# Spreading the count of passed thresholds by VectorE turns in the later searches of a routed feed-forward kernel

## Chip, cores and metric

One core of a Trainium2 chip runs the whole program. The metric is device time in microseconds (us), the median of several runs. TensorE is called PE here, VectorE DVE, ScalarE ACT, GpSimd POOL, SyncE SP.

## What is computed

Attention over 8 batches, 8 heads, 576 positions and 64 features, in which scores more than tau under the row's maximum are dropped, feeds a mixture of 8 experts. Tokens (4608, 512 features) go to experts greedily by the largest logits, with room for 576 tokens in each expert:

```python
scores = scale * np.matmul(q, k.transpose(0, 1, 3, 2))
scores = np.where(scores >= np.max(scores, -1, keepdims=True) - tau, scores, -1e9)
x = softmax(scores) @ v                      # as (4608, 512)
logits = x @ w_gate                          # (4608, 8)
for idx in np.argsort(-logits.flatten()):    # greedy
    tok, e = idx // 8, idx % 8
    if assigned[tok] >= 0 or counts[e] >= 576: continue
    assigned[tok] = e; counts[e] += 1
for e in range(8):
    h = np.maximum(x[assigned == e] @ w1[e], 0.0)
    out[assigned == e] = h @ w2[e]
```

## The kernel before

The attention takes the first half of the time. Then eight rounds follow, each for the expert that fills up next: a search finds the threshold at which some expert has 576 takers among the tokens that are left, the tokens of that expert are compacted into a list, gathered from memory (`xg`), scaled and transposed by PE (`turn`, L821, into `pt`), split into a high and a low part (`xh` by ACT, `xl` by DVE), and go through two layers of matmuls (L880 for the first, L912 for the second) with weights that are split in the same way (`w1h`, `w1l`, `w2h`, `w2l`; the low parts are DVE subtractions). The hidden layer `H` is split as well. Round r+1's search runs beside round r's or round r-1's matmuls.

A search has seven levels, -1 to 5. At each, `step_cmp` compares all 128x36 best logits with up to 32 thresholds (DVE, `cmp`, 1152 columns); `step_cnt` counts them by expert in nine small matmuls (L496) and takes the counts out of PSUM (`cn`, or from the fourth search on four small DVE operations on `cs`); `step_flag` sets a flag for each threshold that some expert passes with at least 576 (`jka`, written as a column of `fla`: one flag on each of the first 32 partitions); `step_n` needs the number of flags, on all 128 partitions. It gets it by a PE product of `fla` with a matrix of ones (L545, levels -1 and 0) or with `hb`, which holds the width of a level's step (L531, levels 1 to 5), into the PSUM tile `rps`. DVE reads it there: at levels -1 and 0 in `jk`, which picks the threshold out of `E`, and at levels 1 to 4 in `sd`, the running sum of steps that the next level's `cmp` adds. The first search (`alone`) runs at the end of the attention and uses other PSUM tiles; searches 2 and 3 (`s.count<=ADDS`, ADDS is 3) sum the counts by another PE product; searches 4 to 7 sum them on DVE. The eighth round needs no search.

The order of instructions on each engine is fixed when the program is built. A planner holds a clock for PE (advanced by fixed amounts for each matmul of the feed-forward, plus `held` for products of the search) and, in the class `Vec`, one for DVE (each operation adds a time by its size). The search is a generator: where it yields `gap()`, the planner goes on placing feed-forward matmuls on PE until `V.wait()` has passed, that is until DVE's planned work is done plus a margin `V.lat`, which is `LATS[r]` for the search of round r (counted from 0; the third search has LATS[2]). At each gap, `s.fill()` puts one deferred DVE subtraction (`w1l`, `w2l`, low part of `H`) into DVE's queue; others are put there when they are older than AGE (7 us of the planner's clock), or when a matmul that needs them is placed. So at run time each engine works its own queue in order, and waits where the planner's clocks were off. The gather of a round's tokens goes to POOL's queue, the loads of weights to SP's. The `x` of round r is made once round r-1's first layer is done and 8 us (6.5 in round 1) of the planner's clock after the gather was issued; the search of round 2 stands still from round 1's `take` until round 1's `x` is done.

Of the kernel before, what the change touches and what calls it, by code (L numbers as in the profile page):

```python
# [9 lines left out]
F32 = mybir.dt.float32  # L10
F32R = mybir.dt.float32r
BF16 = mybir.dt.bfloat16
I32 = mybir.dt.int32
AF = mybir.ActivationFunctionType
ALU = mybir.AluOpType
AX = mybir.AxisListType
# [395 lines left out]

class Vec:

    def __init__(s,e): s.e=e; s.free=0.0; s.now=0.0; s.lat=LAT; s.fix=0.125
    def after(s,t): s.free=max(s.free,t)
    def ease(s): return max(0.0,s.free-s.now-0.4)
    def wait(s): return max(0.0,s.free-s.now)+s.lat
    def __getattr__(s,n):
        f=getattr(s.e,n)  # L420
        def g(out,*a,**k):
            src=k.get("in_",a[0] if a else out)
            big=max((int(np.prod(x.shape[1:])) for x in (out,src) if hasattr(x,"shape")),default=1)
            s.free=max(s.free,s.now)+s.fix+big/(0.96 if n!="tensor_tensor" or out.dtype!=BF16 or src.dtype!=BF16 else 1.9)/1000
            return f(out,*a,**k)  # L425
        return g
LAT=0.25

class Router:
# [77 lines left out]
    def step_flag(s,lv):  # L507

        V=s.V
        if s.count>ADDS: n=s.cn[:,3]  # L510
        else:
            n=s.ps()[0:32,0:8]
            if s.count>2: s.T.matmul(n,s.sum,s.cn,start=True,stop=True)
            else:
                for c in range(4): s.T.matmul(n,s.eye[:,32*c:32*c+32],s.cn[:,8*c:8*c+8],start=(c==0),stop=(c==3))
        if lv==1: V.tensor_scalar(s.st,s.st,s.lo,None,op0=ALU.add)
        jk=s.wk.tile([32,9],BF16,name="jka"); s.jk=jk; m=s.js
        fl=jk[:,8:9] if lv==5 else s.fl[0:m,lv+1:lv+2]
        V.tensor_scalar(jk[0:m,0:8],n[0:m],CAP-0.5,None,op0=ALU.is_ge,op1=ALU.max,accum_out=fl)
    def step_n(s,B):  # L520

        V=s.V
        lv=B["lv"]
        ps=s.ps()
        if lv>0:


            d=ps[:,0:1]
            for l in range(lv,0 if s.alone else lv-1,-1):
                k=32 if l==5 else 128  # L530
                s.T.matmul(d,s.hb[0:k,l-1:l].to_broadcast([k,128]),s.jk[:,8:9] if l==5 else s.fl[:,l+1:l+2],start=(l==lv),stop=(l==1 or not s.alone))  # L531
            if not s.alone and lv<5:
                sd=s.wk.tile([128,1],F32,name="sd",bufs=3)
                if lv==1: V.tensor_copy(sd,d)
                else: V.tensor_tensor(sd,B["add"],d,op=ALU.add)
                d=sd
            if lv<5: return {"add":d,"lv":lv+1}
            s.T.matmul(ps[:,1:10],s.ones[0:32],s.jk,start=True,stop=True)
            lo=s.wk.tile([128,1],F32,name="lo5",bufs=2)
            if s.alone: V.tensor_tensor(lo,s.lo,d,op=ALU.add)  # L540
            else: V.scalar_tensor_tensor(lo,d,B["add"],s.lo,op0=ALU.add,op1=ALU.add)
            return {"lo":lo,"lv":6,"full":ps}
        E2=s.wk.tile([128,J+2],F32,name="E",bufs=3)
        n=ps[:,0:1]
        s.T.matmul(n,s.ones,s.fl[:,lv+1:lv+2],start=True,stop=True)  # L545
        sm=s.wk.tile([128,2],F32,name="sm",bufs=3); lo=sm[:,0:1]
        jk=s.wk.tile([128,J+2],F32,name="jk2")
        V.scalar_tensor_tensor(jk,s.k("io"),n,B["E"],op0=ALU.is_equal,op1=ALU.mult,accum_out=lo)
        if lv==-1:

            V.tensor_scalar(E2,s.k("pw"),lo,FMAX,op0=ALU.mult,op1=ALU.min)
            V.scalar_tensor_tensor(E2,s.k("nw"),lo,E2,op0=ALU.mult,op1=ALU.max)
        else:
            s.ab=sm[:,1:2]
            V.scalar_tensor_tensor(s.ab,lo,-1.0,lo,op0=ALU.mult,op1=ALU.max)
            V.tensor_scalar(E2,s.k("io4"),s.ab,lo,op0=ALU.mult,op1=ALU.add)
        return {"E":E2,"lo":lo,"lv":lv+1}
# [86 lines left out]
    def phase(s,last=False):  # L644

        s.stage="search"; V=s.V
        def held(t): s.pe=t; V.after(V.now+t+0.2)
        if s.first: s.prep(31)
        else:
            yield V.ease()  # L650
            s.prep()
            yield V.ease()
        s.alone=s.first; s.first=False
        s.count+=1
        if last:

            lo=s.wk.tile([128,1],F32,name="lo"); V.memset(lo,-FMAX/4); E={"lo":lo}
        else:
            E={"E":s.k("E1"),"lv":-1}
            def gap():  # L660

                w=V.wait(); s.fill()
                return w
            s.on=True
            for i in range(7):
                s.step_cmp(E); yield gap()
                held(0.34); s.step_cnt(); yield gap()
                if s.count<=ADDS: held(0.16)
                s.step_flag(E["lv"]); yield gap()
                held(0.1); E=s.step_n(E)  # L670
                if not s.alone: yield V.ease()
            s.on=False
        s.pick(E)
        if last:
            yield V.wait()
            held(0.13); s.pick2()
        s.stage="pick"; s.rank1(E)
        yield V.wait()
        held(0.2); s.rank2()
# [14 lines left out]
        yield V.wait() if alone else 0.35  # L694
        s.idx=s.compact2(cps)

LATS=[0.15,0.35,0.7]+[0.8]*5; FIX=(0.125,0.15)
GA=[5.0,6.5,8.0,8.0]; AGE=7.0; HALF=1; WARM=[30,6,64]
W1Y=1.0; W1X=8.5; L2O=(0,4,1,2,3); L2Z=1; HFB=3; RW=[0.2,0.4,0.4,0.4]; LOWP=(); LPF=7; LOWT=1.4; PREPW=1; WLY=(1.0,1.0)

def moe(ctx,tc,R,start,xrows,w1,w2,out,ident):
    nc=tc.nc
    V=R.V; A=nc.scalar; G=nc.gpsimd; T=nc.tensor
    E,D,F=w1.shape
# [16 lines left out]
    def flush():  # L721
        while True:
            if fills and (clk[0]-fills[0][0]>AGE or (not R.on and V.free<=clk[0]+0.2)): pull()
            yield 0.3
# [63 lines left out]
    def rows(r,s):  # L788
        while r>0 and ("x",r-1) not in done: yield 0.5
        order=(4,0,1,2,3) if 0<r<=HALF else range(5)  # L790
        for t in order:
            n=128 if t<4 else 64
            x=wk.tile([128,XW],F32,name="xg",bufs=5); s["xg",t]=x
# [17 lines left out]
        def parts(t):  # L811
            ps=s["xps",t]
            if r==0: return (lambda n: s[n][:,:,128*t:128*t+128] if t<4 else s[n][:,:,512:576]),ps if t<4 else ps[:,:,:64]
            if t<4: return (lambda n: s[n][:,:,128*t+32*(t//2):128*t+32*(t//2)+128]),ps
            return (lambda n: s[n].rearrange("p k (a b) -> p k a b",a=2)[:,:,:,256:288]),ps[:,:,:64].rearrange("p k (a b) -> p k a b",a=2)
        def turn(t):
            n=128 if t<4 else 64
            ps=R.cp().rearrange("p (d n) -> p d n",d=4) if r==0 and t==4 else pt.tile([128,4,128],F32,name="pt")
            s["xps",t]=ps
            held[0]+=0.5  # L820
            for d in range(4): T.transpose(ps[:,d,:n],s["xg",t][:n,d*128:(d+1)*128],ident[:n,:n])  # L821
            xv,pv=parts(t); A.activation(xv("xh"),pv,AF.Copy)  # L822
        def low(t):
# [106 lines left out]
    def place():  # L930
        for r in range(8):
            while r>2 and ("l2",r-3) not in done: yield 0.5
            s=st[r]={}
            if r==0: yield start[1]
            V.now=clk[0]; V.lat=LATS[r]; V.fix=FIX[r>0]
            def steps(g):
                for d in g:
                    held[0]+=R.pe+(0.09 if R.pe else 0.0); R.pe=0.0
                    yield d
                    while ("take",1) in done and ("x",1) not in done: yield 0.2  # L940
                    V.now=clk[0]
                    if R.stage=="pick" and "ei" not in s:
                        s["ei"]=R.e
                        jobs.append([clk[0],w1_load(r,s)]); jobs.append([clk[0]+0.1,w2_load(r,s)])
                held[0]+=R.pe+(0.09 if R.pe else 0.0); R.pe=0.0
                if "ei" not in s:
                    s["ei"]=R.e
                    jobs.append([clk[0],w1_load(r,s)]); jobs.append([clk[0]+0.1,w2_load(r,s)])
            yield from steps(start[0] if r==0 else R.ahead if r==1 else R.phase(r==7))
            if r<2:  # L950
                yield from packing(r,s)
                while "ahead" not in done: yield 0.1
            else:
                if r<7: R.close()
                jobs.append([clk[0],packing(r,s)])
                yield 0.1
    def packing(r,s):
        while r==1 and not {("w2",0),("hl",0,7)}<=done:
            if fills: pull()
            yield 0.1  # L960
        for d in R.pack(r==0,r<2):
            held[0]+=R.pe+(0.09 if R.pe else 0.0); R.pe=0.0
            yield d
            V.now=clk[0]
        s["idx"]=R.idx
        jobs.append([clk[0],rows(r,s)])
    clk=[0.0]; held=[0.0]; jobs=[[0.0,place()],[0.0,flush()]]
    def run(limit):
        while jobs:
# [88 lines left out]
```

## Time and profile before

| | |
|---|---|
| median of 3 runs | 969.45 us (968.88 to 969.48) |
| the profiled execution | 973.53 us |
| its span, first to last instruction | 971.8 us |
| mean granted clock of PE | 0.991 |

The profile is of one execution, which took 4.08 us more than the median; 1.7 us of it lie around the span. In its rows a matmul's time is from its start to its modelled end, so that consecutive ones overlap; what one costs is read from the starts. The attention ends near 475 us, and the feed-forward of round 0 starts near 492, round 1 at 557, round 2 at 620, round 3 at 682, round 4 at 741, round 5 at 800, round 6 at 858 and round 7 at 911. Search 3 runs from 539 to 592 us, search 4 from 598 to 646, and the last level of search 7 ends near 809.

### The profile page before, as it was taken

The numbers are of one execution on the slowest core, as the hardware profiler recorded it, in microseconds if no ns is written. First come the engines' busy times: TensorE is split into PE (matmuls) and PEld (weight loads), VectorE is DVE, ScalarE is ACT, GpSimd is POOL, SyncE is SP. The second block draws the span as 40 slices with busy tenths as digits, with TensorE's granted clock in tenths as the row PEclk, the third lists the DMA queues.
The fourth block names the chain that finished last, engine by engine and source line by source line (L and its number), as shares of the span: only waits on it lengthen the run. The fifth ranks groups of instructions, "written<-read, shape, count | busy, mean of one in ns | idle before, by whom it ended". The sixth has DMA issues, their size and how long they took to land.

```text
span 971.8 us, 24256 instructions
## 1 busy us (share of the span) xinstructions
PE 939.9 (97%) x9170; PEld 704.4 (72%) x9170; DVE 775.4 (80%) x2177; ACT 637.9 (66%) x1301; POOL 277.3 (29%) x485
## 2 busy tenths in 40 slices
PE   7999999999999999998889999899999999999996
PEld 4566656565566656565789797797988979798994
DVE  7999999999999999996678778788796978736220
ACT  5999999999999999995545353443543435445330
POOL 2435344353434343340010302303132210510101
PEclk9999999999999999999999999899999999999999
DMA  6232253533432333205752504425351432841101
GB/s 257 100 115 94 85 181 104 196 133 105 172 109 102 123 106 117 87 2 197 247 176 71 191 18 137 141 88 170 102 157 41 139 128 99 258 134 39 39 11 43
DMA packets 36436, 117.00 MB, mean 120 GB/s; under 512 B 4448, under 2 KB 5088, under 8 KB 35808
## 3 DMA queue, kind: packets, MB, share of 16 engines
q1 hardware_dynamic: 28928, 93.89, 27.9%
q0 software_dynamic: 5888, 19.03, 6.3%
q10 hardware_dynamic: 1504, 2.54, 0.8%
q8 instruction: 72, 1.18, 0.5%
q14 instruction: 44, 0.36, 0.1%
HBM read 93.01 MB, written 21.38 MB: 118 GB/s over the span
## 4 chain that ended last, share of the span: by engine, by line
PE 90%; DVE 5%; issue 2%; DMA 2%; ACT 1%; POOL 0%; POOLq 0%; ACTq 0%; DVEq 0%
PE pf L880 22%; PE pf L912 21%; PE sc L69 15%; PE xo L155 14%; PE tb L98 8%; PE sc L98 2%; PE pt L821 2%; PE xo L165 2%; DVE z L74 1%; DVE pp L90 1%; PE rps L496 1%; PE xo L177 1%; PE xo L246 1%; DVE cmp L425 1%; DMA out_dram<-y,idx 1%
## 5 line engine op out<-in xcount | busy, mean ns | idle before, releaser
L74 DVE TENSOR_SCALAR_CACHE_REDUCE z<-sc 128x576 f32<-128x576 f32 x288 | 206.0, 752 | 17.3 <-PE sc L69 15.3
L75 POOL TENSOR_SCALAR nb<-nb,taub 128x1 f32<-128x1 f32 x288 | 144.9, 504 | 250.4 <-DVE z L74 189.3
L86 ACT ACTIVATE pp<-z,nb 128x576 f32<-128x576 f32 x256 | 193.1, 773 | 26.6 <-DVE z L74 23.1
L90 DVE SCALAR_TENSOR_TENSOR pp<-z,nb,pp 128x576 f32<-128x576 f32 x256 | 199.9, 813 | 0.0
L912 PE MATMUL pf<-w2h,H 128*128 128x512 f32 x576 | 191.0, 398 | 0.5 <-DVE H L425 0.5
L69 PE MATMUL sc<-qk 64*128 64x288 f32 (+1 forms) x1280 | 180.2, 426 | 1.3 <-DVE z L74 1.0
L155 PE MATMUL xo<-pt,vt 128*64 128x320 f32 (+1 forms) x1024 | 155.7, 420 | 0.0
L116 ACT ACTIVATE pt<-tb 128x512 f32<-128x512 f32 x253 | 137.5, 590 | 2.0 <-PE tb L98 1.4
L912 PE MATMUL pf<-w2l,H 128*128 128x512 f32 x320 | 127.2, 398 | 0.0
L920 POOL DMA_INDIRECT out_dram<-y,idx x40 | 47.8, 1196 | 266.2 <-ACT y L915 207.7
L912 PEld LDWEIGHTS pf<-w2h,H 128*128 128x128 f32 x576 | 106.9, 188 | 21.0 <-DVE H L425 0.9
L69 PEld LDWEIGHTS sc<-qk 64*128 64x128 f32 (+1 forms) x1280 | 94.6, 180 | 29.0 <-DVE z L74 4.4
L880 PE MATMUL pf<-xl,w1h 128*128 128x288 f32 (+2 forms) x512 | 111.6, 302 | 1.4 <-DVE xl L425 1.4
L880 PE MATMUL pf<-xh,w1h 128*128 128x288 f32 (+2 forms) x512 | 110.9, 302 | 1.3 <-ACT xh L822 1.3
L880 PE MATMUL pf<-xh,w1l 128*128 128x288 f32 (+2 forms) x512 | 111.1, 302 | 0.0
L98 PEld LDWEIGHTS tb<-ident,pp 64*128 64x128 f32 x2032 | 75.4, 140 | 44.6 <-issue 18.9
L155 PEld LDWEIGHTS xo<-pt,vt 128*64 128x64 f32 x1024 | 60.7, 136 | 58.4 <-issue 32.4
L915 ACT ACTIVATE y<-pf 128x512 f32<-128x512 f32 x40 | 23.9, 598 | 119.4 <-PE pf L912 115.8
L892 ACT ACTIVATE hf<-pf 128x576 f32<-128x576 f32 x56 | 36.5, 651 | 94.5 <-PE pf L880 78.5
L98 PE MATMUL tb<-ident,pp 64*128 64x64 f32 x2032 | 91.9, 227 | 3.1 <-ACT pt L116 3.0
L794 POOL DMA_INDIRECT xg<-xrows,idx x40 | 47.7, 1192 | 161.4 <-PE rps L496 81.2
L880 PEld LDWEIGHTS pf<-xh,w1h 128*128 128x128 f32 x512 | 83.2, 191 | 1.9 <-ACT xh L822 1.5
(209 smaller groups left out, 1356.9 us busy)
## 6 DMA issues: line engine op xcount, KB each, us to landing
qk<-qk_dram SPq DMA_DIRECT2D x31, 864.0 KB, 5.4
vt<-vl_dram SPq DMA_DIRECT2D x32, 576.0 KB, 3.8
w2s<-w_dram SPq DMA_DIRECT2D x32, 512.0 KB, 6.7
w1s<-w_dram SPq DMA_DIRECT2D x28, 512.0 KB, 5.7
xrows<-pp SPq DMA_DIRECT2D x24, 260.0 KB, 2.5
xts<-xt SPq DMA_DIRECT2D x2, 1152.0 KB, 5.1
pt<-xts SPq DMA_DIRECT2D x2, 1152.0 KB
xrows<-xr SPq DMA_DIRECT2D x8, 260.0 KB, 2.8
```

Source lines behind the costliest of these rows:

```text
L69: T.matmul(sc[o,f,:HS], kd["q",h][r,c], kd["k",h][r,:],start=True,stop=True)
L74: V.tensor_scalar(z,SC.pop(t)[:,:,:HS],-0.125,None,op0=ALU.mult,op1=ALU.min,accum_out=nb[:,0:1])
L75: G.tensor_scalar(nb[:,1:2],nb[:,0:1],taub[:,0:1],None,op0=ALU.add)
L86: A.activation(pview(t),ZB[t].rearrange("p a b -> p (a b)"),AF.Exp,bias=NBI[t][:,0:1],scale=-1.0)
L90: V.scalar_tensor_tensor(pv,ZB.pop(t).rearrange("p a b -> p (a b)"),NBI[t][:,1:2],pv,op0=ALU.is_le,op1=ALU.mult,accum_out=den_of(p)[:,p%4/ ...
L98: g=slice(64*r,64*r+64); T.transpose(o[:,r],x[r%len(x)][g],ident[g,g])
L116: else: A.activation(o,tb,AF.Copy)
L155: T.matmul(xo[64*h:64*h+64,:q.stop-q.start],v[:,f,128*u+64*h:128*u+64*h+64],PT[p][:,h,u,q],start=new,stop=last,skip_group_check=True)
L794: G.indirect_dma_start(out=x[:n],out_offset=None,in_=xrows,in_offset=IOA(ap=s["idx"][:n,t:t+1],axis=0))
L880: T.matmul(ps[:,h,:n],s[w][:,k,f*128:(f+1)*128],s[x][:,k,cols[h]],start=(i==0),stop=(i==11))
L912: T.matmul(ps[:,0,:],H[:,f,c:c+128],s[w][:,f],start=(f==0 and j==0),stop=e)
L920: G.indirect_dma_start(out=out,out_offset=IOA(ap=s["idx"][:n,t:t+1],axis=0),in_=y[:n],in_offset=None)
```

## The change

In searches 4 to 7, `step_n` at levels -1 to 4 no longer issues the PE product. The new function `spread` makes four DVE turns (transposes) of the flag column, read 32 times over as a 32x32 block, into the four groups of 32 rows of a 128x32 tile: each row then holds all 32 flags. One DVE operation sums them along the row, at levels 1 to 4 times the width of the step (`s.ab` times a constant), so that `hb` is not used there. Level 5 keeps its products. The gap and the held time between `step_flag` and `step_n` go at these levels.

The planner's clock of DVE is changed for all searches: a fixed 0.07 us and the size's time (0.09 more with an accumulator), with 0.115 us of latency before a result counts as done, where it had 0.125 (first search) or 0.15 us fixed and no latency; which operand sets the size is read differently. The margins LATS are cut, and so is the time held for each product (0.09 to 0.05) and each transposed tile (0.5 to 0.45).

```diff
 class Vec:
-    def __init__(s,e): s.e=e; s.free=0.0; s.now=0.0; s.lat=LAT; s.fix=0.125
-    def after(s,t): s.free=max(s.free,t)
+    def __init__(s,e): s.e=e; s.free=0.0; s.done=0.0; s.now=0.0; s.lat=LAT; s.last=None
+    def after(s,t): s.free=max(s.free,t); s.done=max(s.done,t)
     def ease(s): return max(0.0,s.free-s.now-0.4)
-    def wait(s): return max(0.0,s.free-s.now)+s.lat
+    def wait(s): return max(0.0,s.done-s.now)+s.lat
     def __getattr__(s,n):
         f=getattr(s.e,n)
         def g(out,*a,**k):
-            src=k.get("in_",a[0] if a else out)
-            big=max((int(np.prod(x.shape[1:])) for x in (out,src) if hasattr(x,"shape")),default=1)
-            s.free=max(s.free,s.now)+s.fix+big/(0.96 if n!="tensor_tensor" or out.dtype!=BF16 or src.dtype!=BF16 else 1.9)/1000
+            ins=[x for x in (*a,*k.values()) if hasattr(x,"tensor")]
+            big=max(int(np.prod(x.shape[1:])) for x in (out,*ins[:1]))
+            twice=n=="tensor_tensor" and out.dtype==BF16 and ins[0].dtype==BF16
+            t=max(s.free,s.now)
+            if any(x.name==s.last for x in ins): t=max(t,s.done)
+            acc=k.get("accum_out"); s.last=(out if acc is None else acc).name
+            s.free=t+0.07+big/(1.9 if twice else 0.96)/1000+(0.0 if acc is None else 0.09)
+            s.done=s.free+0.115
             return f(out,*a,**k)
...
+    def spread(s,lv):
+        V=s.V; x=s.fl[0:32,lv+1:lv+2].to_broadcast([32,32])
+        t=s.wk.tile([128,32],BF16,name="tt"); n=s.wk.tile([128,1],F32,name="tn",bufs=3)
+        for c in range(4): V.transpose(t[32*c:32*c+32],x)
+        if lv<1: V.tensor_reduce(n,t,axis=AX.X,op=ALU.add)
+        else:
+            u=s.wk.tile([128,32],F32,name="tu")
+            V.scalar_tensor_tensor(u,t,s.ab,s.k("lew")[:,lv-1:lv].to_broadcast([128,32]),op0=ALU.mult,op1=ALU.mult,accum_out=n)
+        return n
     def step_n(s,B):
...
-        ps=s.ps()
+        if s.count>ADDS and lv<5: d=s.spread(lv)
+        else: ps=s.ps()
         if lv>0:
+            if s.count>ADDS and lv<5:
+                if lv>1: sd=s.wk.tile([128,1],F32,name="sd",bufs=3); V.tensor_tensor(sd,B["add"],d,op=ALU.add); d=sd
+                return {"add":d,"lv":lv+1}
...
-        n=ps[:,0:1]
-        s.T.matmul(n,s.ones,s.fl[:,lv+1:lv+2],start=True,stop=True)
+        if s.count>ADDS: n=d
+        else: n=ps[:,0:1]; s.T.matmul(n,s.ones,s.fl[:,lv+1:lv+2],start=True,stop=True)
...
-                s.step_flag(E["lv"]); yield gap()
-                held(0.1); E=s.step_n(E)
+                s.step_flag(E["lv"])
+                if s.count<=ADDS or E["lv"]==5: yield gap(); held(0.1)
+                E=s.step_n(E)
...
-LATS=[0.15,0.35,0.7]+[0.8]*5; FIX=(0.125,0.15)
+LATS=[0.15,0.35,0.35]+[0.6]*5
...
-            held[0]+=0.5
+            held[0]+=0.45
...
-                    held[0]+=R.pe+(0.09 if R.pe else 0.0); R.pe=0.0
+                    held[0]+=R.pe+(0.05 if R.pe else 0.0); R.pe=0.0
```

## Rows read from the trace of the kernel before

**Rows 1.** The page: its head and the first part, for PE and DVE (busy us, share of the span, instructions).

```profile
span 971.8 us, 24256 instructions
...
PE 939.9 (97%) x9170; PEld 704.4 (72%) x9170; DVE 775.4 (80%) x2177; ACT 637.9 (66%) x1301; POOL 277.3 (29%) x485
```

**Rows 2.** Windows of single feed-forward stages. Columns: stretch and its length, then busy us (and instructions) of PE, PEld, DVE, ACT, POOL, then the mean granted clock of PE as a share of full speed, the DMA share and GB/s. 741 to 770 is a first layer with a search beside it, 858 to 884 a first layer without one.

```profile
741.00:770.00 29.00, 29.00 (x252) 28.21 (x252) 24.80 (x75) 15.01 (x31) 3.75 (x4) 1.00 0.26 91
...
858.00:884.00 26.00, 26.00 (x195) 25.91 (x194) 11.89 (x24) 15.19 (x31) 2.09 (x2) 1.00 0.29 100
```

**Rows 3.** Windows around the start of the third feed-forward (round 2) and over most of searches 4 to 7, same columns.

```profile
598.00:616.00 18.00, 18.00 (x127) 14.20 (x125) 15.74 (x48) 5.84 (x12) 9.94 (x8) 1.00 0.49 156
616.00:626.00 10.00, 5.61 (x36) 4.67 (x33) 6.98 (x19) 4.38 (x9) 2.24 (x2) 0.66 0.50 180
626.00:820.00 194.00, 194.00 (x1433) 171.12 (x1433) 157.52 (x471) 84.55 (x168) 40.47 (x34) 1.00 0.35 117
```

**Rows 4.** Timeline of PE at the start of the third feed-forward (start us, us, engine, line, operation, count, and in brackets the idle time before and what ended it).

```profile
616.82 0.16 PE L531 MATMUL rps<-fla,hb 128*128 128x1 bf16 x1 [0.35 <-DVE jka L425]
618.15 0.46 PE L821 MATMUL pt<-ident,xg 64*128 64x64 f32 x4 [1.16 <-DVE xl L425]
620.27 0.42 PE L496 MATMUL rps<-oh,cmp 128*128 128x32 bf16 x9 [1.66 <-DVE cmp L425]
...
622.57 0.85 PE L880 MATMUL pf<-xl,w1h 128*128 128x288 f32 x2 [1.22 <-DVE xl L425]
623.22 0.68 PE L880 MATMUL pf<-xh,w1l 128*128 128x288 f32 x2
623.70 0.68 PE L880 MATMUL pf<-xh,w1h 128*128 128x288 f32 x2
```

**Rows 5.** Timeline of DVE in the same stretch.

```profile
618.79 1.42 DVE L425 SCALAR_TENSOR_TENSOR cmp<-st,sd,b 128x1152 bf16<-128x1152 f32 x1
620.13 0.69 DVE L425 TENSOR_TENSOR w2l<-w2s,w2h 128x512 fp32r<-128x512 f32 x1
...
622.09 0.42 DVE L425 TENSOR_TENSOR xl<-pt,xh 128x256 fp32r<-128x256 f32 x1
```

**Rows 6.** Timeline of PE around one product of fla in a full stretch (search 4).

```profile
631.15 0.42 PE L880 MATMUL pf<-xh,w1l 128*128 128x288 f32 x2
631.42 0.18 PE L531 MATMUL rps<-fla,hb 128*128 128x1 bf16 x1
631.46 0.52 PE L880 MATMUL pf<-xh,w1h 128*128 128x288 f32 x2
631.81 0.43 PE L880 MATMUL pf<-xl,w1h 128*128 128x288 f32 x2
```

**Rows 7.** Instructions of the tile fla on PE, after the attention (counts after the x; min/median/max ns; first and last start).

```profile
L531 PE MATMUL rps<-fla,hb x24: 164/178/180, 508.8 to 803.0; 128*128 128x1 bf16 x24
...
L545 PE MATMUL rps<-fla,onesb x12: 177/177/178, 497.5 to 778.3; 128*128 128x1 bf16 x12
```

**Rows 8.** Timeline of DVE through one level of search 4.

```profile
630.13 0.14 DVE L425 TENSOR_SCALAR_CACHE_REDUCE jka<-cs 32x8 bf16<-32x8 f32 x1
...
631.65 0.16 DVE L425 TENSOR_TENSOR sd<-sd,rps 128x1 f32<-128x1 f32 x1 [0.63 <-PE rps L531]
631.84 1.42 DVE L425 SCALAR_TENSOR_TENSOR cmp<-st,sd,b 128x1152 bf16<-128x1152 f32 x1
```

**Rows 9.** Timeline of DVE, small operations: three at the end of search 3, two in the first level of search 4.

```profile
589.42 0.16 DVE L425 TENSOR_REDUCE m<-f 128x1 f32<-128x8 f32 x1
589.61 0.15 DVE L425 TENSOR_SCALAR e<-m 128x1 int32<-128x1 f32 x1
589.68 0.25 DVE L425 SCALAR_TENSOR_TENSOR gm<-qm,m,ge 128x36 bf16<-128x36 bf16 x1
...
603.56 0.26 DVE L425 SCALAR_TENSOR_TENSOR jk<-cst,rps 128x34 f32<-128x34 f32 x1 [0.62 <-PE rps L545]
...
603.86 0.24 DVE L425 TENSOR_SCALAR E<-cst,sm 128x34 f32<-128x34 f32 x1
```

**Rows 10.** Waits of DVE from 598 to 830 us (us in total, times, longest).

```profile
DVE sd L425 <- PE rps L531: 13.7, 13, 3.0
DVE jk L425 <- PE rps L545: 3.9, 6, 1.1
```

**Rows 11.** Timeline of DVE in one level of search 3.

```profile
573.69 1.42 DVE L425 SCALAR_TENSOR_TENSOR cmp<-st,sd,b 128x1152 bf16<-128x1152 f32 x1
...
577.41 0.15 DVE L425 TENSOR_SCALAR_CACHE_REDUCE jka<-rps 32x8 bf16<-32x8 f32 x1 [0.44 <-PE rps L513]
...
578.58 0.15 DVE L425 TENSOR_TENSOR sd<-sd,rps 128x1 f32<-128x1 f32 x1 [0.40 <-PE rps L531]
```

**Rows 12.** Timeline of PE in the same level: the products and the count.

```profile
573.27 0.18 PE L531 MATMUL rps<-fla,hb 128*128 128x1 bf16 x1
...
575.53 0.39 PE L496 MATMUL rps<-oh,cmp 128*128 128x32 bf16 x9
...
578.35 0.18 PE L531 MATMUL rps<-fla,hb 128*128 128x1 bf16 x1
```

**Rows 13.** The chain that ended last, at the end of the attention: row transposes behind the first search (start us, us, what).

```profile
475.44 2.41 PE xo L246 x12
```

**Rows 14.** Waits of PE beside search 2 (us in total, times, longest).

```profile
PE rps L496 <- DVE cmp L425: 1.2, 2, 0.9
```

More of the change, by code (lines that the diff above doesn't have):

```diff
@@ L934, in place @@
             if r==0: yield start[1]
-            V.now=clk[0]; V.lat=LATS[r]; V.fix=FIX[r>0]
+            V.now=clk[0]; V.lat=LATS[r]
             def steps(g):
                 for d in g:
-                    held[0]+=R.pe+(0.09 if R.pe else 0.0); R.pe=0.0
+                    held[0]+=R.pe+(0.05 if R.pe else 0.0); R.pe=0.0
                     yield d
@@ L944, in steps @@
                         jobs.append([clk[0],w1_load(r,s)]); jobs.append([clk[0]+0.1,w2_load(r,s)])
-                held[0]+=R.pe+(0.09 if R.pe else 0.0); R.pe=0.0
+                held[0]+=R.pe+(0.05 if R.pe else 0.0); R.pe=0.0
                 if "ei" not in s:
@@ L961, in packing @@
         for d in R.pack(r==0,r<2):
-            held[0]+=R.pe+(0.09 if R.pe else 0.0); R.pe=0.0
+            held[0]+=R.pe+(0.05 if R.pe else 0.0); R.pe=0.0
             yield d
```

## The prediction

> **What bounds the kernel now.** I read the page's first part, then the windows by stage, then the waits and the timelines of TensorE (PE) and VectorE (DVE). PE is busy 97% of the span and DVE 80% [rows 1]. The windows show where PE's missing share is not: from 626 to 820 us, which holds most of the searches that the change touches, PE is busy 194.00 of 194.00 us, and DVE 157.52 (81%) [rows 3]. A feed-forward stage without a search beside it (858 to 884) has the same full PE with DVE at 11.89 of 26 us; one with a search (741 to 770) takes 29 us and has DVE at 24.80 [rows 2]. So in these stages time is counted in PE's slots: a search costs what it puts into PE's queue, and its own length is hidden as long as its tokens are ready before the round that needs them. That holds for rounds 3 to 5 at least: PE has no stall from 626 to 820.
>
> One stretch is different. Between 616 and 626 us PE is busy only 5.61 us and its granted clock falls to 0.66 of full [rows 3]: here the third feed-forward (round 2) starts and waits. The timeline of PE names the waits: 1.16 us for xl, 1.66 for cmp, 1.22 for xl again [rows 4]; with a 0.35 us one before 616.82 the idle time is about 4.4 us. After it, pairs of matmuls start 0.48 us apart (623.22 to 623.70) [rows 4] where the same pairs start 0.27 apart at full clock (631.15 to 631.42) [rows 6]: about seven pairs at the lower of the two clock levels (1.2 of 2.4 GHz) after an engine that had stood idle, some 7 x 0.21 = 1.5 us more. Together this stretch loses about 5.9 us. DVE is what is late: the last xl of round 2 runs at 622.09, behind cmp of the fourth search (1.42 us) and w2l [rows 5].
>
> **The change, part by part.**
>
> (a) Products removed. Searches 4 to 7 lose the product of fla at levels -1 to 4: 6 x 4 = 24. The trace's 24 products with hb and 12 with ones belong to searches 2 to 7, so 16 and 8 of them go [rows 7]. The price of one is read from starts: pair at 631.15, product at 631.42, next pair at 631.46, next at 631.81 [rows 6]. 631.15 to 631.81 is 0.66 us for two pairs and a product; two pairs alone are 0.53. So 0.13 us each, less than the 0.18 us it shows as busy. 23 of the 24 lie in full stretches (the one at 616.82 is in the stall): 23 x 0.13 = **-3.0 us**, straight off the path, as nothing else there bounds. I see no way for this term to be under 2.5 or over 3.3.
>
> (b) VectorE work added. Each of the 24 steps gets four 32x32 turns and a sum over 32 columns. No turn of this kind is in the trace. Low bound: a small independent operation lets the next one start 0.07 us after it (589.61 to 589.68), plus 32 columns at the 1.42/1152 us of cmp [rows 8], 0.04: 0.11 us. High bound: small operations that follow each other in order start 0.19 apart (e after m at 589.42, 589.61) [rows 9]. Four turns: 0.44 to 0.76 us. The sum with accumulator is nearest to jk: 0.30 us from its start to the next operation's (603.56 to 603.86) [rows 9]; the plain sum of levels -1 and 0 to m: 0.19. So 0.63 to 1.06 us a step, 24 steps: 14 to 25 us more DVE time over some 220 us, less four small copies (0.18 each). DVE goes from 81% to 87 to 92%. I take 0.85 a step, between the ends, as the sources are the same and only the written partitions differ.
> The row shows 0.19 us between dependent operations and 0.07 behind an independent one [rows 9]. The Trainium skill (VectorE: DVE Perf Modes, section on two Vector instructions with no wait between them) says that an instruction whose output starts in another group of 32 partitions than the last output is held until all earlier ones have finished; the four turns write four such groups, so by this rule the high end holds, 25 us more of DVE against the low end's 15, and no run here shows it. The third rival has its chance from the rows' high end, which the rule's result equals.
>
> What hides it: DVE now stands idle for these products, 13.7 us before sd and 3.9 before jk between 598 and 830 us [rows 10]. The way from flag to sum today is 630.13 (jka) to 631.65 (sd) = 1.52 us [rows 8], with other work put in between; the new way is 0.28 + 0.44 to 0.76 + 0.3 = 1.0 to 1.3 us. So a level becomes 0.2 to 0.5 us shorter or, where DVE is crowded, stays as long. For the end that is worth nothing: rounds 3 to 6 do not wait for their searches. One gap a level goes too, and with it one of three places where a deferred subtraction (w1l, w2l, H) is pulled; those go to later places.
>
> (c) The planning clock. LATS of the third search falls from 0.7 to 0.35, of later ones from 0.8 to 0.6; durations now have 0.115 us of latency where they had a larger fixed part. For the third search a level has three such waits: 3 x (0.35 - 0.115) = 0.7 us less a level. The trace shows room for that: in the level 573.27 to 578.35 (5.08 us) cmp ends at 575.11 and its PE group starts at 575.53, jka ends at 577.56 and its product starts at 578.35 [rows 11, 12]. Six levels lie behind the hold on round 1's rows, so pick, gather and x of round 2 come about 6 x 0.7 = 4 us sooner. That is the size of the idle 4.4 us at 616. Against it: in that stretch the fourth search's first two or three spreads lay 0.85 us each on a DVE that is busy 15.74 of 18 us before it [rows 3], in place of idle waits like the 0.62 us before jk at 603.56 [rows 9]. Bounds for the stretch: 0 to 5.9 us gained; I take **-3.5 us**, a bit over half, since DVE's load there is kept and only shifted.
>
> (d) PE placed closer behind DVE. With 0.35 instead of 0.7 the slack of 0.4 to 0.8 us above shrinks to 0.1 to 0.5; where DVE is late PE now waits. 18 places in the third search, 28 in searches 4 to 7 (cmp only): I take **+0.5 us**, bounds 0 to 4.
>
> (e) First search and what ends attention: its planned level grows by about 0.3 us, so one or two more row transposes are planned into it and fewer remain behind (12 matmuls, 2.41 us, on the chain at 475.44 [rows 13]). Gain or loss up to 1.2 us, taken as 0. Held times (0.5 to 0.45, 0.09 to 0.05) only reorder: 0.
>
> **Sum** for the profiled execution, 973.53 us: -3.0 - 3.5 + 0.5 = -6.0, 967.5. The median of the runs is 969.45, 4.1 lower than the profiled one; the change is the same in both, so 963.5 us.
>
> **Rivals.**
> 1. The slots alone: the stall at 616 moves or stays as it is, because xl of round 2 is again put behind the fourth search's cmp. For: DVE was busy through that stretch. Against: the third search's waits are cut most. 969.45 - 3.0 = 966.4.
> 2. PE waits for DVE: slack is cut by more than DVE can keep up with; 18 + 28 places at some 0.07 to 0.13 us give 3 to 6 us, against -3.0 and part of -3.5. No measurable change, 969. For: DVE at 95% in the third search's levels once these take 4.4 us (5.08 less 0.44 and 0.40 idle is 4.2 us of work each [rows 11]). Against: the second search, planned with 0.35 already, made PE wait for cmp only twice, 1.2 us in all [rows 14].
> 3. DVE becomes the bound of rounds 2 to 5. A turn costs 0.19 or more, DVE passes about 92%, the deferred subtractions of w2l and H (six fewer are pulled a search, 0.6 us each, 3.6 us a round) come when PE's second-layer matmuls already ask for them. At half of that, 4 x 1.8 = 7.2 us, less 3.0, is +4.2: 973.6, more if the clock falls again. It decides from the point where DVE's busy share in a search stage such as 741 to 770 (86% now) passes about 97%.
> That the products stay is excluded by the code: searches 4 to 7 take the other branch.
>
> **Chances.** Forecast (slots and a good part of the stall) 0.50, all of it faster; rival 1 0.20, of which 0.17 faster and 0.03 unchanged; rival 2 0.13, unchanged; rival 3 0.17, slower. Faster 0.67, same 0.16, slower 0.17; 0.2%, 1.9 us, is about what a measurement of this kernel can tell from no change. The forecast's own range is 959 to 966.5. The low end of the whole: -3.2 - 5.9 - 1.2 is 959.2, a little wider 958.5; the high end takes in rivals 1 and 2 and the lighter half of rival 3: 972.
>
> **What would show it.** (a) no products of fla with ones or hb beyond those of searches 1 to 3, and pairs of the first layer 0.27 apart through the old places. (b) four turns per step, 0.10 or 0.19 us apart, DVE busy some 15 to 25 us more. (c) the third search's levels 4.3 to 4.5 us apart instead of 5.1, x of round 2 ready near 618, PE's idle time at the start of round 2 under 2 us and the granted clock there near 1.00. (d) PE idle behind cmp and jka in the third search under 1 us in sum. Wrong if DVE's share in the search stages goes to 97% and PE waits for H or w2l (rival 3), or if the third search keeps its length (rival 1).

## The result, and the profile after

The change makes the kernel slower: 974.36 us (median of 5 runs, 972.44 to 977.21) against 969.15 us, a ratio of 1.006 with a 95% interval of 1.0043 to 1.0077. Run again on another occasion it gave 1.0052 (1.0038 to 1.0066). The forecast was 963.5 us, with 958.5 to 972.0 as the range of the whole, and the time lies above it; the third rival had been worked out at 973.6.

The execution profiled after the change was the fastest of its five (972.44 us), and the one whose trace the prediction read was slow for its kernel: a second profile of the kernel before gave 969.02 us. The two traces of before differ only ahead of round 1 (first matmul of round 1 at 557.1 and at 552.6 us); from there to the second layer of round 7 both take 379.7 us, stall included. So kernels are compared below over that stretch, from the first matmul of round 1 to the first of round 7's second layer, and by ratios to before on the same chip.

The page after answers to [rows 1]: one operation kind more on DVE (24 us more busy), 24 matmuls less on PE, nearly the same PE time.

```profile
span 970.7 us, 24326 instructions
...
PE 937.1 (97%) x9146; PEld 702.5 (72%) x9146; DVE 799.3 (82%) x2309; ACT 638.6 (66%) x1301; POOL 268.7 (28%) x485
```

The stretch from round 1 on, by windows: the second profile of the kernel before, the first and the second of the changed one (length, then busy us of PE, PEld, DVE, ACT, POOL, PE's granted clock, DMA share, GB/s).

```profile
552.60:932.30 379.70, 374.80 (x2651) 332.69 (x2650) 270.02 (x755) 166.62 (x330) 80.67 (x68) 0.99 0.33 108
```

```profile
552.00:935.70 383.70, 374.93 (x2627) 334.46 (x2626) 293.07 (x883) 167.07 (x330) 69.49 (x68) 0.99 0.33 107
```

```profile
551.30:937.50 386.20, 377.41 (x2628) 336.40 (x2627) 292.98 (x883) 167.20 (x330) 71.16 (x68) 0.98 0.32 106
```

Length less PE's busy time is PE's idle time: 4.90 us before, 8.77 and 8.79 after. In some places the granted clock is 0.50, the lower level, and half of PE's busy time there is lost: 2.0 us before (one place of 6.8 us, partly idle), 3.4 us (two places of 3.4 us) and 6.3 us after. What is left, PE's own work, is 372.8 before, 371.5 and 371.1 after. So PE's own work falls by 1.3 to 1.7 us, idle time adds 3.9 and the clock 1.4 to 4.3; the clock is what sets the two profiles of the changed kernel apart. Who is late is mostly DVE, as PE's waits in this stretch of the changed kernel (first profile) say:

```profile
PE pf L930 <- DVE H L430: 5.7, 6, 1.8
PE pf L898 <- DVE xl L430: 1.9, 1, 1.9
PE pf L898 <- ACT xh L840: 0.9, 1, 0.9
```

Before, PE never waited for H but once, 0.51 us. The costliest place is the second layer of round 3 (33.3 us from its first matmul to round 4's, 29.9 before). DVE of the changed kernel there, through the first level of search 6:

```profile
707.48 0.81 DVE L430 TENSOR_TENSOR H<-hf,H 128x512 fp32r<-128x512 f32 x2
708.22 0.14 DVE L430 TENSOR_SCALAR_CACHE_REDUCE jka<-cs 32x8 bf16<-32x8 f32 x1
...
708.41 0.85 DVE L430 STREAM_TRANSPOSE tt<-fla 32x32 bf16<-32x32 bf16 x4
709.29 0.19 DVE L430 TENSOR_REDUCE tn<-tt 128x1 f32<-128x32 bf16 x1
709.51 0.26 DVE L430 SCALAR_TENSOR_TENSOR jk<-cst,tn 128x34 f32<-128x34 f32 x1
...
710.38 0.76 DVE L430 TENSOR_TENSOR cmp<-b,E 128x576 bf16<-128x576 f32 x1
711.05 0.89 DVE L430 TENSOR_TENSOR H<-hf,H 128x512 fp32r<-128x512 f32 x2
711.86 1.28 DVE L430 TENSOR_TENSOR xg<-xg 128x512 f32<-128x512 f32 x2
713.18 0.15 DVE L430 COPY cs<-rps 32x8 f32<-32x8 f32 x1
713.37 0.54 DVE L430 TENSOR_TENSOR cs<-cs,rps 32x8 f32<-32x8 f32 x3
713.84 0.81 DVE L430 TENSOR_TENSOR H<-hf,H 128x512 fp32r<-128x512 f32 x2
```

and of the kernel before (second profile) at the same level:

```profile
707.20 0.81 DVE L425 TENSOR_TENSOR H<-hf,H 128x512 fp32r<-128x512 f32 x2
707.93 0.14 DVE L425 TENSOR_SCALAR_CACHE_REDUCE jka<-cs 32x8 bf16<-32x8 f32 x1
...
708.01 0.81 DVE L425 TENSOR_TENSOR H<-hf,H 128x512 fp32r<-128x512 f32 x2
709.45 0.26 DVE L425 SCALAR_TENSOR_TENSOR jk<-cst,rps 128x34 f32<-128x34 f32 x1 [0.62 <-PE rps L545]
```

Before, DVE did another low part of H while PE made the product, and still stood idle 0.62 us. After, the gap is gone and the spread stands there; the H of 708.01 has moved to 711.05, behind cmp, and the one after it (711.06 before) to 713.84, behind two xg and cs. PE, in the changed kernel, is there first:

```profile
711.86 0.51 PE L930 MATMUL pf<-w2h,H 128*128 128x512 f32 x1 [0.44 <-DVE H L430]
...
714.57 1.10 PE L930 MATMUL pf<-w2h,H 128*128 128x512 f32 x2 [1.41 <-DVE H L430]
715.47 0.63 PE L930 MATMUL pf<-w2l,H 128*128 128x512 f32 x1
715.89 0.63 PE L930 MATMUL pf<-w2h,H 128*128 128x512 f32 x1
```

715.47 to 715.89 is 0.42 us for a matmul that takes 0.23 at full speed: in the window from 712 to 718 us the granted clock is 0.73, the lower level for part of it, after an engine that had stood idle. The stage windows that answer to [rows 2] and to the forecast's point of 97% show DVE far from it, 88% and 92%, though the second one holds such a wait:

```profile
741.00:770.00 29.00, 29.00 (x250) 28.07 (x249) 25.40 (x84) 15.49 (x33) 3.02 (x4) 1.00 0.26 91
770.00:800.00 30.00, 29.13 (x173) 23.39 (x172) 27.65 (x88) 10.15 (x20) 8.50 (x8) 1.00 0.41 135
```

The stall at the start of round 2 ([rows 4, 5]) is still there. DVE and PE of the changed kernel, first profile:

```profile
614.40 0.85 DVE L430 STREAM_TRANSPOSE tt<-fla 32x32 bf16<-32x32 bf16 x4
615.29 0.25 DVE L430 SCALAR_TENSOR_TENSOR tu<-tt,sm,cst 128x32 f32<-128x32 bf16 x1
...
615.58 0.16 DVE L430 TENSOR_TENSOR sd<-tn 128x1 f32<-128x1 f32 x1
615.78 1.42 DVE L430 SCALAR_TENSOR_TENSOR cmp<-st,sd,b 128x1152 bf16<-128x1152 f32 x1
617.12 0.41 DVE L430 TENSOR_TENSOR xl<-pt,xh 128x256 fp32r<-128x256 f32 x1
```

```profile
617.59 0.54 PE L898 MATMUL pf<-xl,w1h 128*128 128x288 f32 x2 [1.88 <-DVE xl L430]
```

The last xl now stands behind the spread, sd and cmp, 2.7 us in all. With the new planning alone, without the spread, it is done 3 us earlier:

```profile
613.97 0.42 DVE L430 TENSOR_TENSOR xl<-pt,xh 128x256 fp32r<-128x256 f32 x1
```

DVE's own waits for the products, from round 1 to the second layer of round 7, are in the kernel before (second profile, first two lines) 19.5 us; in the changed kernel this one line is left (us in total, times, longest):

```profile
DVE sd L425 <- PE rps L531: 15.4, 17, 2.9
DVE jk L425 <- PE rps L545: 4.1, 7, 1.1
```

```profile
DVE jk L430 <- PE rps L562: 0.2, 1, 0.2
```

So the spread did go where DVE had waited. Searches 4 to 7 did not get shorter by it: from the first cmp of a search to its last they take 41.1, 39.8, 41.7 and 39.1 us in the changed kernel (161.7 in all), where the kernel before takes 154.1 (second profile) and the new planning alone 148.9.

### The profile page after: what moved, and what is told of

It is laid out like the page before. It is cut to its first block, busy times and chain, and to the rows that moved or that the text cites. A ratio compares the mean times of both kernels' runs of the same rounds, so it can differ in the third digit from the quotient of the medians.

```text
span 970.7 us, 24326 instructions
## 1 busy us (share of the span) xinstructions
PE 937.1 (97%) x9146; PEld 702.5 (72%) x9146; DVE 799.3 (82%) x2309; ACT 638.6 (66%) x1301; POOL 268.7 (28%) x485
## 4 chain that ended last, share of the span: by engine, by line
PE 83%; DVE 12%; issue 2%; DMA 2%; ACT 0%; POOLq 0%; POOL 0%; SPq 0%; DVEq 0%; ACTq 0%
PE pf L898 20%; PE pf L930 17%; PE sc L69 15%; PE xo L155 14%; PE tb L98 8%; PE sc L98 2%; PE xo L165 2%; DVE cmp L430 2%; PE pt L839 2%; DVE H L430 1%; DVE pp L90 1%; DVE z L74 1%; PE rps L501 1%; PE xo L177 1%; DMA out_dram<-y,idx 1%
## 5 line engine op out<-in xcount | busy, mean ns | idle before, releaser
L938 POOL DMA_INDIRECT out_dram<-y,idx x40 | 45.0, 1124 | 275.4 <-ACT y L933 177.7
L812 POOL DMA_INDIRECT xg<-xrows,idx x40 | 42.1, 1051 | 160.5 <-PE rps L501 80.3
```

Of the source, the lines that this page charges most:

```text
L812: G.indirect_dma_start(out=x[:n],out_offset=None,in_=xrows,in_offset=IOA(ap=s["idx"][:n,t:t+1],axis=0))
L938: G.indirect_dma_start(out=out,out_offset=IOA(ap=s["idx"][:n,t:t+1],axis=0),in_=y[:n],in_offset=None)
```

## The experiments

Edits are shown against the kernel named with them. "New clock" means the changed planning: the new durations, LATS and held times.

**Second profiles.** Both kernels unchanged. The first:

> The kernel before, unchanged, for a second profile. Its timed runs (968.4 to 969.5 us) lie 4 us under the execution whose trace I read (973.5). Theory A (that execution had a stall which the timed ones mostly lack: the one at 616 us or a late start of round 0): the new trace shows round 0 starting near 489 instead of 492 us or less than 4.4 us of idle time of PE near 616, and a time near 969. Theory B (a profiled execution is always some 4 us slower): again about 973.5, with the same stall.

969.04 us; its trace has round 0 at 490.1, round 1 at 552.6 and the stall at the start of round 2 whole (0.35, 1.16, 1.66 and 1.22 us, now from 612 to 618). Both theories fell in part: a profiled execution is not slower as such, and the 4 us lay ahead of round 1, not in the stall.

> The changed kernel, unchanged, for a second profile. Its runs spread from 972.4 to 977.2 us with clocks from 0.993 to 0.988. Theory D (VectorE is late with the low parts of H at the second layers of rounds 1 to 5): ratio to before near 1.005, and where this execution is slower than 972.4 it waits longer for H or at the lower clock behind such waits. Theory P (the planning clock alone, in searches 2 and 3): the extra time lies between 490 and 620 us.

Ratio 1.0052 (1.0038 to 1.0066). The waits for H are those of the first profile to 0.05 us; the execution loses 3 us more at the lower clock, 1.7 of it behind the wait of 1.84 us for H in round 1 (behind the same wait the first profile loses none) and the rest behind the stall of round 2. As theory D had it.

**The two halves of the change, each alone.** First the new clock without the spread:

```diff
-        if s.count>ADDS and lv<5: d=s.spread(lv)
+        if s.count>SPREAD and lv<5: d=s.spread(lv)      # SPREAD=99; so in the other branches, and the gap
```

> The new planning clock with the products of TensorE kept in all searches (no spread; the gap and its pull of a deferred subtraction stay). Theory D (the spread's VectorE time and the lost pulls make the low parts of H late): 966 to 970 us, PE waits for H under 1 us in all. Theory P (the shorter margins and the new durations themselves make PE wait): 973 to 976 us, the same waits for H as in the changed kernel.

965.9 us, ratio 0.9972 (0.996 to 0.9985), and in a second run, the reference for other kernels, 0.9967 (0.9955 to 0.9979):

> The new planning clock with all products kept, once more, as the reference for the other kernels of this chip. 0.996 to 0.9985 of before, that is 965 to 970 us by chip; from the start of round 1 to the second layer of round 7 near 376.8 us, with about 2 us of idle time of PE.

376.8 us from round 1 on with 2.0 us idle, nearly all one wait of 1.85 us for H in the second layer of round 1 (theory D had under 1 us, and a time from 966 on):

```profile
556.00:932.80 376.80, 374.79 (x2651) 332.29 (x2650) 269.27 (x751) 166.97 (x330) 74.91 (x68) 1.00 0.33 109
```

Then the spread with the old clock (class Vec, LATS, FIX and held times of before):

> The spread by VectorE turns with the old planning clock (old durations, LATS 0.7 and 0.8, old held times). Theory D: slower than before, 971 to 978 us, PE waits for H at second layers. Theory P: 966 to 967 us, before less the 3 us of the removed products.

974.21 us, ratio 1.0058 (1.0044 to 1.0072); 11.8 us idle, but here 8.7 of it for xl and xh and only 1.9 for H. So the planning clock gains and the spread loses; theory P is out.

**What in the spread costs.** Four kernels, the first three on one chip, the fourth on another. A turn charged at its measured time:

```diff
             s.done=s.free+0.115
+            if n=="transpose": s.free=t+0.215; s.done=s.free+0.02
```

> The changed kernel with one edit of the planning clock: a turn counts 0.215 us, as the trace shows it (0.85 us for four), in place of 0.103. Theory M (the planner takes the spread for 0.45 us shorter than it is, so that everything behind it in VectorE's queue is late): 967 to 970 us, waits for H under 1 us. Theory W (the VectorE work itself, and the pull that is lost with the gap, make the low parts of H late): 972 to 975 us.

1.0011 (1.0002 to 1.002): between the theories in time (972.3, where before took 971.43), 4 parts in 1000 under the changed kernel. PE is idle 6.6 us instead of 8.8, waits for H fall from 5.7 to about 4 us. A part of the loss goes when the turn is charged rightly.

```diff
-                if s.count<=ADDS or E["lv"]==5: yield gap(); held(0.1)
+                yield gap()
+                if s.count<=ADDS or E["lv"]==5: held(0.1)
```

> The changed kernel with the gap between flag and spread kept in searches 4 to 7, so that a deferred subtraction is pulled there as before. Theory G (the lost pulls delay w2l and the low parts of H): 967 to 970 us, hardly any wait for H at the second layers. Theories M and W without it: 972 to 976 us, or worse, since the search gets longer.

1.0013 (1.0004 to 1.0022), again between: 6.8 us idle, H still late in rounds 1 to 5 by 0.5 to 1.8 us. With the products kept and the spread done beside them, its result unused (new clock):

```diff
+        if s.count>ADDS and lv<5: s.spread(lv)
```

> The new planning clock with all products and gaps kept, and the spread done beside them in searches 4 to 7 with its result unused: 24 spreads more on VectorE, nothing else changed. Against the same kernel without them (965.9 us): theory W (VectorE's time is what costs): +3 to +8 us, 969 to 974. Theory G (the lost pulls): within 1 us, 965 to 967.

1.0018 (1.0008 to 1.0028), where the new clock alone gave 0.9972 and 0.9967: 4.6 to 5.1 parts in 1000, about 4.5 to 5 us, with no pull lost: in the range of theory W. But "nothing else changed" does not hold: the planner counts the unused spread as well, and the traces show the other instructions in another order, on DVE and on PE, than in the new clock's kernel. The same with the turns on the same partitions (four blocks of a 32-row tile; the edit's main line):

```diff
-        for c in range(4): V.transpose(t[32*c:32*c+32],x)
+        for c in range(4): V.transpose(s.tz[:,c],x)     # the sum then reads one block, on 32 rows
```

> Like the kernel with the unused spread, but the four turns write four blocks on the same 32 partitions instead of four groups of partitions, and the sum runs on 32 partitions. Theory H (a turn costs 0.21 us because its output starts in another group of 32 partitions than the last one's): four turns take 0.45 to 0.55 us instead of 0.85, 24 x 0.35 = 8 us less VectorE time, and the idle time of PE from round 1 on falls from 5.5 us to between 2 and 4.5. Rival (a turn takes 0.21 us anyway): the same 0.85 us and the same idle time of PE.

Four turns take 0.47 us instead of 0.85. The turns of the changed kernel, then of this one (count, min/median/max ns, with the four of one step):

```profile
L430 DVE STREAM_TRANSPOSE tt<-fla x96: 199/202/208, 593.0 to 802.7; 32x32 bf16<-32x32 bf16 x96
```

```profile
L430 DVE STREAM_TRANSPOSE tz<-fla x96: 156/157/201, 595.8 to 807.5; 32x32 bf16<-32x32 bf16 x96
...
771.27 0.47 DVE L430 STREAM_TRANSPOSE tz<-fla 32x32 bf16<-32x32 bf16 x4
```

Theory H holds for the turn: starts 0.21 us apart when the written partitions change, some 0.1 when they don't. PE's idle time fell from 5.5 to 4.5 us, at the edge of what it said, and the time by less than the measurement tells: 1.0014 (1.0004 to 1.0025). This pair says more. Apart from the turns and the sum, both kernels have the same instructions in the same order on DVE and on PE, and DVE has 10.6 us less to do in the second; windows and PE's waits for H, the unused spread first, then this kernel:

```profile
555.50:937.40 381.90, 376.38 (x2652) 332.03 (x2651) 291.92 (x887) 167.40 (x330) 68.78 (x68) 1.00 0.32 108
...
PE pf L931 <- DVE H L430: 4.4, 4, 1.8
```

```profile
553.40:934.10 380.70, 376.16 (x2651) 331.89 (x2650) 281.32 (x887) 167.40 (x330) 69.72 (x68) 1.00 0.32 108
...
PE pf L932 <- DVE H L430: 4.3, 4, 1.8
```

The stretch is 1.2 us shorter, and the four waits for H are the same to 0.05 us, at the same places (1.8, the new clock's own, then 0.9, 0.3 and 1.3 us). So the length of the turns is not what makes these H late. What the two kernels share is the order of the queues; what that order costs without any turn was not run.

**The price of a product.** Each of the 24 issued twice (new clock, products kept; the product with ones likewise):

```diff
-            for l in range(lv,0 if s.alone else lv-1,-1):
+            for l in [*range(lv,0 if s.alone else lv-1,-1)]*(2 if s.count>ADDS and lv<5 else 1):
```

> The new planning clock with products kept, and each of the 24 products of searches 4 to 7 at levels -1 to 4 issued twice with the same result. If one costs its slot of 0.13 us on the path, as I priced it: 24 x 0.13 = +3.1 us against 965.9, about 969. If the slot is hidden (PE's time is not what bounds there): within 0.5 us of 965.9.

0.9986 (0.9977 to 0.9996), 1.4 to 1.9 parts in 1000 over the new clock's two runs on other chips, between the two expectations; by the traces 377.4 us from round 1 on against 376.8: +0.6 us, 0.03 each. It does not settle what the first of two costs: one issued right behind another may spare what breaking into the stream costs. It shows that the 0.13 us is not the product itself.

**The third search's margin alone**, in the kernel before:

```diff
-LATS=[0.15,0.35,0.7]+[0.8]*5
+LATS=[0.15,0.35,0.35]+[0.8]*5
```

> The kernel before with one number changed: the margin of the third search, 0.35 instead of 0.7. My step (c): the third search's levels come 4.3 to 4.5 us apart instead of 5.1, x of round 2 is ready some 4 us sooner, PE's idle time at the start of round 2 falls from 4.4 to under 2 us: 964 to 967 us (0.995 to 0.998 of before). Rival (the gain of the new planning clock comes from its durations, not from this margin): 0.999 to 1.002 of before, with the stall in place.

0.9942 (0.9918 to 0.9965), a little better than forecast, and once more as a reference:

> The kernel before with the third search's margin at 0.35, once more, as the reference: 0.992 to 0.9965 of before, no idle time of PE from round 1 on.

961.08 us, 0.9918 (0.9905 to 0.993): 5.6 us less by the first run, 8 by the second. In both profiles the stretch from round 1 on is 7.6 us shorter than before (372.1 against 379.7), more than the 5.9 I had as the bound for the stall. PE has no idle time there that shows and no clock under full:

```profile
552.70:924.90 372.20, 372.20 (x2643) 331.06 (x2643) 267.30 (x747) 166.59 (x330) 73.74 (x68) 1.00 0.33 110
```

The products of search 3 (L513) say why, first the kernel before (second profile), then this one: the last of seven starts at 582.9 and at 573.7; the levels behind the hold are 5.15 and 4.16 us apart.

```profile
L513 PE MATMUL rps<-c8n,sum x7: 167/168/173, 540.3 to 582.9; 128*32 128x8 f32 x7
```

```profile
L513 PE MATMUL rps<-c8n,sum x7: 167/168/172, 539.5 to 573.7; 128*32 128x8 f32 x7
```

This version, one number of the kernel before, is the fastest of all that ran.

**The spread where PE has no other wait.** On that kernel, without and with the gap:

> The same with the spread in searches 4 to 7 (gap gone), a turn counted at 0.18 us. If the spread loses by itself (VectorE work of 1.0 us in each level in place of a wait, and one pull less): 4 to 7 us over the reference, PE waiting for H and for x at the starts of layers. If it loses only together with the stalls of the other planners: 1 to 3 us under the reference, the slots of 24 products.

> As the one before with the gap kept in searches 4 to 7, so that three deferred subtractions a level are pulled, and a turn counted at 0.21 us. If the lost pull is what makes H late: within 1 us of the reference or under it. If VectorE's time is: 3 to 6 us over it.

969.9 us, 1.0017 (1.0008 to 1.0026), 8.8 us over the reference; with the gap 972.21 us, 1.0039 (1.0025 to 1.0054), 11 us over it: both more than any of the theories had. Without the gap DVE has 24 us more work, PE is idle 6.2 us (2.8 for H, 3.3 for xh and xl) and loses 5.1 at the lower clock, while its own work is 2.0 us less (370.1 against 372.1):

```profile
553.90:935.30 381.40, 375.22 (x2619) 335.07 (x2618) 291.45 (x879) 166.91 (x330) 68.74 (x68) 0.99 0.33 108
```

With the gap PE is idle 9.0 us: 4.5 of that for H, 4.2 for cmp of a search that has become longer. So the spread loses by itself, and the lost pull is not what decides: kept, it helped under the new clock and hurt under the old.

**Where only one search has it.** New clock, a turn charged rightly, the spread in search 7 alone (SPREAD=6):

> The new planning clock, a turn counted at 0.215 us, and the spread in search 7 alone: 6 products go instead of 24, and 6 x 1.0 us of VectorE work is added beside rounds 4 and 5. If VectorE's time is the price wherever it is spent: 1 to 2 us over the new planning clock alone. If it is only where rounds 2 and 3 are crowded: equal to it or 0.5 us less.

0.9972 (0.9962 to 0.9983) against 0.9967 for none, on one chip: no gain that can be told, with one wait for H of 0.66 us more than the new clock alone has. The dearer theory's 1 us is within the measurement.

## Why the prediction was wrong, by its steps

(a) The products. They are gone: after the attention `fla` has 8 and 4 products left of the 24 and 12 of [rows 7], those of searches 2 and 3. The term of -3.0 us was over-sized: between kernels of the same planning PE's own work fell by 1.6 and 2.0 us (new clock, 373.1 without the spread), 2.0 (third search's margin alone) and 2.5 (old clock), so 0.07 to 0.10 us each. That figure may hide waits too short to show: with the spread unused and all products kept, own work is 374.6, 1.5 us over the new clock's. Reading 0.13 from [rows 6] may take the whole irregularity around one product for its price.

(b) The spread's size was right, its price was not. 23 us more DVE time in the stretch, where I had 14 to 25; the turn came out at 0.21 us, just over my high end. The Trainium skill (VectorE: DVE Perf Modes, two Vector instructions with no wait between them) says that an instruction whose output starts in another group of 32 partitions than the last output is held until the earlier ones have finished, and the runs agree: with the four groups of 32 partitions the turns take 0.85 us, on one group 0.47.

**The step that failed is "What hides it".** I let the spread go into DVE's waits for the products, had a level of the search 0.2 to 0.5 us shorter or as long as before, and gave the added work no term on the path. The waits did go, 19.5 us of them, and the way from flag to sum (start of jka to start of jk or sd) did get shorter, from 1.57 us on average with the new clock alone to 1.3 or 1.4. But that way had held a deferred subtraction as well, and "those go to later places" had a price that I put at nothing: they stand elsewhere in the same queue, and a level of searches 4 to 7 became 0.5 us longer than with the new clock alone (161.7 against 148.9 us for 24). DVE works its queue in order, and behind the spread and what follows it stand an H, an xl or a cmp that PE is about to ask for. The whole came out, what the products saved taken off, at 7.8 us under the new clock (1.0052 against 0.9972 of before), 5 under the old, 8.8 on the kernel without stalls. That the spread loses is shown under three plannings. How much of it is DVE's time and how much the changed order of its queue stays open: with the turn charged rightly, or with the gap kept, about half of the 7.8 went, and with the unused spread shorter turns alone gave 1.2 us.

(c) The third search was sped up about as worked out: 4.53 us a level in the changed kernel (I had 4.3 to 4.5), its last product from 582.9 to 576.8, where I had 4 us. But x of round 2 was not sooner: its last xl runs at 617.12, before at 617.63 (second profile). With the new clock alone it runs at 613.97, so what the third search gave, the fourth's spreads and the low parts queued with them took. Alone, the same margin is worth 5.6 to 8 us. So the -3.5 was far too small for (c) by itself and too large beside (b): the sum added two steps that share DVE's queue around 610 us.

(d) PE waits of the third search for cmp did not come; instead one wait of 1.85 us for H in round 1's second layer, in every kernel with the new clock, and in every profile but the first of the changed kernel 1.7 us lost at the lower clock behind it. The term of +0.5 was too small by 1.3 to 3 us. The kernel before with only the third search's margin cut does not have it, so it belongs to the rest of the new planning (durations, held times, the other margins); which of these was not tried. From round 1 on, the margin alone takes 372.1 us and the whole new planning 376.8.

(e) Fewer row transposes are left behind the first search, 8 instead of 20. Round 0 starts at 488.1 and 488.8 us in the changed kernel, at 490.1 in before (second profile); but over all profiles it is 488.1 to 490.8 with the new planning and 489.1 to 492.3 with the old, so a gain is not shown.

Rival 3, with 0.17, is nearest to what happened: PE waits for H. That its 973.6 is near the time is luck in part, since its +4.2 holds neither the 2.7 us that the new planning gains by itself nor the stall that stayed. Its point of decision was wrong: not a busy share of 97% in a stage, but one place or two per round where H or xl is asked for within a microsecond or two of being made.

## What to carry to other kernels

Work that is moved to an engine with idle time is not free, even where it takes the place of a wait: look at what else had been done in that wait, at what stands behind it in that engine's queue, and when its reader asks for it. Terms of a sum that pass through the same queue at the same time can't be added; here a margin worth 5.6 to 8 us and 24 products worth about 2 came, together with the spread and the rest of the planning, to a loss of 5. And split a change into its planning and its work before judging either: one margin, set for one search, was worth more than all the rest.

## What the runs showed of the hardware

Small DVE operations that write another group of 32 partitions than the one before start 0.21 us apart, on the same group about 0.1 us (0.85 and 0.47 us for four). A second small product right behind a first costs PE 0.03 us. Idle stretches of PE of 1.4 us and of 1.9 us were followed in these traces by matmuls at the lower clock level in some places (715.47 in the changed kernel) and not at once in others (617.96 to 618.74, full speed, then slower). The same wait of 1.85 us in round 1 of the changed kernel was followed by 3.4 us at a granted clock of 0.50 in its second profile and by none in its first: the same program lost 3.4 us to the clock in one execution and 6.3 in another.
